# A gated recurrence and a sine MLP on one core: keys and queries transposed by DMA, weights cast by DMA on the Pool queue, decay factors kept in PSUM, gate phases in a new order on ACT

## The chip, the cores and the metric

The kernel runs on one core of one Trainium2 chip. The metric is the device time of one execution in microseconds (us). The core has five engines with instruction queues of their own: PE (matrix products), ACT (table functions), DVE and POOL (elementwise work) and SP (here only DMA issues). DMAs move data between HBM and SBUF, or within SBUF; matrix products land in PSUM.

## The reference

Four batches, eight heads, 768 steps and 48 dimensions per head. A recurrence per head keeps a 48x48 state that decays by a gate and takes in one outer product a step; its outputs, 3072 rows of 384, go through an MLP with a sine in the middle.

```python
f = 1.0 / (1.0 + np.exp(-f_logit))
for t in range(S):
    state = f[:, :, t, :, None] * state + np.einsum('bhd,bhe->bhde', k[:, :, t], v[:, :, t])
    y[:, :, t] = np.einsum('bhd,bhde->bhe', q[:, :, t], state)
...
h = x @ w_in                                 # 384 -> 2048
s = np.sin(alpha * h)
g = h + s * s / (alpha + 1e-09)
return (g @ w_out).astype(np.float32)        # 2048 -> 384
```

## The kernel before, in words

**Chunks and pairs.** The 768 steps are cut into 6 chunks of 128 (c = 0 to 5). A chunk of two batches, 16 heads, is a *pair* u = 2c or 2c + 1; there are 12. A pair's f, k, q and v come by one DMA each (`load`, 384 KB in pieces of 192 bytes), all on SP's queue in the order of the program, into rings of 3 buffers each. At most eight DMAs of a queue are under way, since the ninth waits for the first one's semaphore.

**The gate phase of a pair** (`pre`). ACT takes exp and ln of f (tiles `f`, `lf`, lines 317 and 320); PE forms running sums with a triangular mask (`cs`, line 342) and column sums (line 345); ACT takes exp of both signs, `Gi` (line 355) and `G` (line 351); then kh = k * Gi and qh = q * G (line 358, `mul`) are formed on POOL or DVE. exp and ln sit in another table of ACT than the sine, so each stretch of gate phases among the sines costs two table loads (line 602).

**Attention of a chunk and batch** (`attend`). PE transposes kh and qh, eight blocks of 128x128 (`tp`, line 398), DVE or ACT copies them to SBUF (`tr`, line 402), PE forms scores (`aps`, line 409), DVE masks them (`at`, line 413), PE adds the state's part (line 419) and the chunk's own (line 427) into `y`, and DVE or ACT casts that into `xT` (line 433), the MLP's input, transposed. `kv` and `st` (lines 439 to 447) carry the state to the next chunk; the decay for that is the last four columns of `G`. Heads are padded from 48 to 64 rows: xT has four blocks of 128 rows, and `spread` (line 474, six small DMAs on SP) moves the rows of block 1 into the gaps of the other three, so that the first layer needs three products. Chunk 0 isn't spread; it uses a fourth product with a weight tile `w_one_bf` of its own (line 495).

**The MLP** (`first`, `second`). Per 128 hidden features: `h` on PE (line 492), the sine on ACT (`s`, line 499), the square on POOL, DVE or ACT (`s2`, line 507), `g` on DVE (line 512). Chunk 0 goes in two halves of 256 columns, the others in 512. The second layer (`o`, line 528) sums 16 products per batch, then a copy (`osb`, line 536) and a store (line 539).

**The weights.** w_in comes in ten DMAs on the queues of SP and ACT as f32 into staging tiles `wi`, the rows of the heads in block 1 twice (for `w_one_bf`), 3.93 MB in all; w_out (3.15 MB) in four on SP. ACT and DVE cast them to bf16 (lines 273 and 289).

**What sets the order.** Every piece of work is an `Op` with a rank, a duration for each engine that may do it, the ops it depends on and the ring buffers it takes. `in_order` places them one by one: of all that could start, the one with the earliest start (plus `BIAS`), then the lowest rank. It writes the program of each engine; at run time each engine works its list off in that order and waits by semaphores. Two lists are fixed ahead: the loads, and `act_order`, the order of gate phases and sines on ACT. `MID` and `PRE34` say after which sine of chunks 0 and 1 a pair's gate phase comes; from chunk 1 on two pairs come after the eighth sine. `LAG` is the delay of the second layer's rank.

Of the kernel before, what the change touches and what calls it, by code (L numbers as in the profile page):

```python
# [16 lines left out]
N_H, N_A, NQ, NV, NG, LAG = 3, 3, 6, 4, 22, 10  # L17
SPX = "SP"
MID = {(0, 15): ([2], [-30]), (1, 7): ([3], [-20])}
PRE34 = ([4], [-10])  # L20
TR_ACT, Y_ACT = True, True
MULS = {"POOL": 1000, "DVE": 560}
BIAS = {"ACT": 600, "DVE": 200, "POOL": -300}
# [22 lines left out]
TABLE_LOAD, DMA_LATENCY, DMA_AHEAD = 1280, 1900, 4000  # L46


def in_order(ops, lines):
# [4 lines left out]
    dma_free, table = 0, None  # L54
# [23 lines left out]
    while left:  # L78
        best = None
        for o in pending:  # L80
# [5 lines left out]
            for e, dur in o.engs.items():  # L86
                s = max(t, free[e])
                if o.dma:
                    s = max(s, dma_free - DMA_AHEAD)
# [4 lines left out]
        if best is None:  # L94
            raise RuntimeError("no operation can start: " + "; ".join(
                f"{o.rank} {o.engs} {o.line and turn[o]} {nth} {[(n, len(b.ring.taken)) for b in o.takes for n in [b.ring.n]]}"
                for o in pending if SPX not in o.engs))
# [3 lines left out]
        if o.dma:  # L101
            dma_free = max(s + 600, dma_free) + o.dma
            o.end = dma_free + DMA_LATENCY
# [18 lines left out]
def kernel(  # L122
# [18 lines left out]

    nc = tc.nc
# [10 lines left out]
    BLK = (0, 2, 3)  # L153
# [12 lines left out]
    wst = pool("wst", 4)  # L166
# [14 lines left out]
    act_order, load_order = [], []  # L181

    def op(rank, engs, emit, deps=(), takes=(), holds=(), table=None, dma=None):
        o = Op(rank, engs, emit, [d for d in deps if d is not None], list(takes), table, dma)
        for b in list(takes) + list(holds):
# [5 lines left out]
        f=3, k=3, q=3, v=3, lf=2, qh=NQ, kh=NQ, vb=NV, G=6, Gi=4, a=N_A, tr=3, at0=3, at1=3, xT=2,  # L191
        h=N_H, s=3, s2=3, g=NG, o=2, osb=3, w=4).items()}
# [5 lines left out]
    qh_b = [consts.tile([C, HP, 2, E], BF16, name=f"qh{i}") for i in range(NQ)]  # L198
    kh_b = [consts.tile([C, HP, 2, E], BF16, name=f"kh{i}") for i in range(NQ)]
# [13 lines left out]
                            pattern=[[-1, FB]], channel_multiplier=1)  # L213
    ones_c = consts.tile([C, 1], BF16)
    nc.gpsimd.memset(ones_c, 1.0)
    for i in range(max(NQ, NV)):
        for ts in (lf_b, qh_b, kh_b, v_b):
            if i >= len(ts):
                continue
            if ts is v_b:  # L220
                nc.vector.memset(ts[i][:, :, :, 0:2, D:], 0.0)
                nc.vector.memset(ts[i][:, :, :, 2:4, 0:16], 0.0)
            else:
                t = ts[i] if ts is not lf_b else ts[i].rearrange("c p b r e -> c (p b) r e")
                nc.vector.memset(t.rearrange("c a r e -> c (a r) e")[:, :, D:], 0.0)
# [408 lines left out]
```

## Time and profile before

| | |
|---|---|
| median of 3 runs | 273.51 us (272.41 to 274.02) |
| the profiled execution | 272.08 us |
| its span, first to last instruction | 270.4 us |
| mean granted PE clock | 0.941 of full speed |
| busy: PE, DVE, ACT, POOL | 217.1, 171.0, 153.3, 139.7 us |
| DMA | 31.48 MB, of it 25.96 MB read from HBM |

A row of the profile is a group or a stretch. In a timeline the columns are start, time, engine, line, operation, result<-operands, count, and in brackets the idle time ahead of it with what ended it. In the chain of waits they are start, time, engine and line. In a group by shape the last column but one is busy time in all and mean ns of one instruction; PE's single durations overlap, so that runs of several in the chain (x8) tell more of their pace. Engine names with a q (SPq) are queues that issue DMAs; such a row lasts as long as the queue took for it, and grows when the rings are full. In the busy table by stretches the last three columns are the granted PE clock, the mean share of the 16 DMA engines in use, and GB/s.

### The profile page before, as it was taken

The numbers are of one execution on the slowest core, as the hardware profiler recorded it, in microseconds if no ns is written. First come the engines' busy times: TensorE is split into PE (matmuls) and PEld (weight loads), VectorE is DVE, ScalarE is ACT, GpSimd is POOL, SyncE is SP. The second block draws the span as 40 slices with busy tenths as digits, with TensorE's granted clock in tenths as the row PEclk, the third lists the DMA queues.
The fourth block names the chain that finished last, engine by engine and source line by source line (L and its number), as shares of the span: only waits on it lengthen the run. The fifth ranks groups of instructions, "written<-read, shape, count | busy, mean of one in ns | idle before, by whom it ended". The sixth has DMA issues, their size and how long they took to land.

```text
span 270.4 us, 4819 instructions
## 1 busy us (share of the span) xinstructions
PE 217.1 (80%) x1785; PEld 124.7 (46%) x1785; DVE 171.0 (63%) x296; ACT 153.3 (57%) x236; POOL 139.7 (52%) x154
## 2 busy tenths in 40 slices
PE   0650358896987879568999969999889999989994
PEld 0430235664564545244555545555555555435542
DVE  2661227768749777658766496856697667765641
ACT  4211475668276685594554975457956577555610
POOL 6400062656135456367428493547685656578830
PEclk9999999997599999975999986999979999999999
DMA  9999999999999669049920399710000001010111
GB/s 144 206 245 182 159 212 370 192 176 196 188 185 219 91 154 141 0 87 198 178 81 0 91 156 187 109 61 31 31 2 15 30 32 58 13 60 3 58 61 58
DMA packets 106295, 31.48 MB, mean 116 GB/s; under 512 B 100176, under 2 KB 105792, under 8 KB 105792
## 3 DMA queue, kind: packets, MB, share of 16 engines
q1 hardware_dynamic: 105920, 29.20, 59.5%
q10 hardware_dynamic: 320, 1.97, 3.5%
q8 instruction: 14, 0.23, 0.4%
q14 instruction: 9, 0.07, 0.1%
q0 software_dynamic: 32, 0.01, 0.0%
HBM read 25.96 MB, written 4.72 MB: 113 GB/s over the span
## 4 chain that ended last, share of the span: by engine, by line
PE 32%; DVE 15%; POOL 12%; ACT 11%; DMA 11%; issue 11%; SPq 5%; POOLq 1%; ACTq 0%; DVEq 0%
PE h L492 12%; POOL s L507 12%; PE o L528 9%; DVE qh L358 6%; DMA wi<-in_moe_w_in_dram 6%; SPq L237 4%; PE y L427 4%; DMA q<-in_q_dram 3%; DVE tr L402 3%; DMA v<-in_v_dram 3%; ACT lf L320 3%; ACT f L317 2%; ACT L602 2%; DVE at L413 2%; ACT s L499 2%
## 5 line engine op out<-in xcount | busy, mean ns | idle before, releaser
L507 POOL TENSOR_TENSOR s<-s 128x512 f32<-128x512 f32 (+1 forms) x112 | 102.3, 928 | 66.4 <-ACT s L499 63.6
L499 ACT ACTIVATE s<-h,al_p 128x512 f32<-128x512 f32 (+1 forms) x112 | 67.8, 626 | 50.7 <-PE h L492 37.5
L492 PE MATMUL h<-xT,w_in_bf 128*128 128x512 bf16 (+1 forms) x336 | 84.3, 365 | 15.2 <-ACT w_in_bf L273 8.9
L512 DVE SCALAR_TENSOR_TENSOR g<-s,al_r,h 128x512 bf16<-128x512 f32 (+1 forms) x112 | 73.4, 667 | 34.7 <-POOL s L507 33.7
L528 PE MATMUL o<-w_out_bf,g 128*128 128x384 bf16 x384 | 81.0, 327 | 1.5 <-DVE g L512 0.6
L358 POOL TENSOR_TENSOR kh<-k,Gi 128x384 bf16<-128x384 f32 x24 | 27.7, 1180 | 52.5 <-ACT Gi L355 52.5
L492 PEld LDWEIGHTS <-w_in_bf 128*128 128x128 bf16 x336 | 32.0, 101 | 42.4 <-ACT w_in_bf L273 10.7
L528 PEld LDWEIGHTS <-g 128*128 128x128 bf16 x384 | 36.1, 98 | 30.5 <-DVE g L512 2.5
L358 DVE TENSOR_TENSOR qh<-q,G 128x384 bf16<-128x384 f32 x19 | 21.8, 1189 | 21.1 <-ACT G L351 15.2
L413 DVE TENSOR_TENSOR at<-aps,mask 128x512 bf16<-128x512 f32 x48 | 30.8, 681 | 4.2 <-PE aps L409 4.0
L427 PE MATMUL y<-at,vb 128*64 128x128 bf16 x192 | 21.0, 261 | 2.2 <-DVE at L413 2.1
L602 ACT ACT_TABLE_LOAD x15 | 19.2, 1283 | 0.3
L433 ACT CAST xT<-y 128x512 bf16<-128x512 f32 x15 | 8.8, 585 | 18.5 <-PE y L427 18.1
L409 PE MATMUL aps<-tr 64*128 64x128 bf16 x192 | 13.4, 253 | 6.8 <-DVE tr L402 5.6
L427 PEld LDWEIGHTS <-vb 128*64 128x64 bf16 x192 | 13.7, 129 | 10.6 <-issue 9.2
L398 PE MATMUL tp<-ident,kh 128*128 128x128 bf16 x96 | 11.0, 248 | 7.8 <-POOL kh L358 6.2
L536 DVE COPY osb<-o 128x384 f32<-128x384 f32 x17 | 9.2, 553 | 9.4 <-PE o L528 9.3
L355 ACT ACTIVATE Gi<-cs 128x384 f32<-128x384 f32 x24 | 12.0, 499 | 4.4 <-PE cs L345 4.4
L409 PEld LDWEIGHTS <-tr 64*128 64x128 bf16 x192 | 7.2, 106 | 13.1 <-DVE tr L402 7.4
L495 PE MATMUL h<-xT,w_one_bf 128*128 128x256 bf16 x32 | 9.7, 304 | 3.4 <-DVE w_one_bf L273 3.4
L351 ACT ACTIVATE G<-cs 128x388 f32<-128x388 f32 x24 | 12.2, 510 | 0.0
L317 ACT ACTIVATE f<-f 128x768 f32<-128x768 f32 x12 | 10.1, 838 | 3.5 <-DMA f<-in_f_logit_dram 3.4
(53 smaller groups left out, 172.6 us busy)
## 6 DMA issues: line engine op xcount, KB each, us to landing
f<-in_f_logit_dram SPq DMA_DIRECT2D x12, 384.0 KB, 6.7
k<-in_k_dram SPq DMA_DIRECT2D x12, 384.0 KB, 6.7
q<-in_q_dram SPq DMA_DIRECT2D x12, 384.0 KB, 6.2
v<-in_v_dram SPq DMA_DIRECT2D x12, 384.0 KB, 6.7
out_dram<-osb SPq DMA_DIRECT2D x24, 192.0 KB, 1.9
wo<-in_moe_w_out_dram SPq DMA_DIRECT2D x4, 768.0 KB, 7.8
wi<-in_moe_w_in_dram SPq DMA_DIRECT2D x2, 512.0 KB, 9.3
wi<-in_moe_w_in_dram ACTq DMA_DIRECT2D x2, 512.0 KB, 9.9
```

Source lines behind the costliest of these rows:

```text
L317: nc.scalar.activation(out=tl["f", u], in_=tl["f", u], func=Act.Exp, scale=-1.0)
L351: nc.scalar.activation(out=tl["G", m], in_=tl["cs", m][:, :H * D + HP], func=Act.Exp, scale=-1.0)
L358: engine[e].tensor_mul(dst[bufs["qh" if dst is qh_b else "kh", m].place % NQ][:, :, :, :D], tl[n, u][:, i * H:(i + 1) * H, :].rearrange("c ...
L409: nc.tensor.matmul(aps[r][:, p, :], t[halves[r], p, :], t[halves[r], HP + p, :], start=True, stop=True)
L413: nc.vector.tensor_mul(a, tl[x, "a"][r], mask4)
L427: nc.tensor.matmul(tl[x, "y"][halves[r], p, :], v_b[bufs["vb", u].place % NV][:, i, r, p, :], tl[x, "at", r][:, p, :], start=(first and p ...
L492: nc.tensor.matmul(h[:, :n], w_in_bf[:, kb, fs], xT[:, BLK[kb], ts], start=(kb == 0), stop=(kb == KB - 1 and whole))
L499: nc.scalar.activation(out=s[:, :n], in_=tl[x, "h"][:, :n], func=Act.Sin, scale=al_p[:, fb:fb + 1])
L507: engine[e].tensor_mul(s2[:, :n], s[:, :n], s[:, :n])
L512: nc.vector.scalar_tensor_tensor(tl["g", c, fb][:, ts], tl[x, "s2"][:, :n], al_r[:, fb:fb + 1], tl[x, "h"][:, :n], Alu.mult, Alu.add)
L528: nc.tensor.matmul(tl["o", c, t], tl["g", c, fb][:, t * P:(t + 1) * P], w_out_bf[:, fb, :], start=(fb == 0), stop=(fb == FB - 1))
L602: nc.scalar.preload_act_table_set(now)
```

## The change

- **Transposes.** For chunks 1 to 5, `tp` on PE and the copy `tr` are replaced by one DMA on SP per chunk and batch (`dma_start_transpose`, 256 KB in bf16, from SBUF to SBUF), 20 in all. kh and qh now share one tile `qk`. Chunk 0 keeps PE.
- **Weights.** 20 DMAs on POOL's queue write bf16 straight into `w_in_bf` (16, by halves of the columns) and `w_out_bf` (4); staging tiles and casts go.
- **Chunk 0's fourth product.** Block 1's rows are placed by PE: shifted copies of the values (`v1_b`, formed by DVE) give three products per batch and half head in place of one (line 422 of the new kernel), so that xT of chunk 0 has three blocks and `w_one_bf` goes.
- **Decay factors.** `G` is written over `cs` in PSUM; the query product reads it there, now on DVE alone; a small copy `gl` keeps the four columns for the state. The last chunk forms no column sums.
- **Order.** `PHASES` lists how many sines stand between the gate phases of which pairs, `RANK` gives each pair's rank, attention has its own delay `ATT`, `LAG` grows from 10 to 50, the first-layer products are kept in order (`h_order`), and durations and biases are new.

The core of the diff:

```diff
-N_H, N_A, NQ, NV, NG, LAG = 3, 3, 6, 4, 22, 10
-MID = {(0, 15): ([2], [-30]), (1, 7): ([3], [-20])}
-PRE34 = ([4], [-10])
-MULS = {"POOL": 1000, "DVE": 560}
-BIAS = {"ACT": 600, "DVE": 200, "POOL": -300}
+N_H, N_A, NQ, NV, NG = 3, 3, 6, 4, 22
+LAG = 50
+ATT = 12
+PHASES = [("pre", [0]), ("sin", 1), ("pre", [1, 2]), ("sin", 21), ("pre", [3]), ("sin", 4), ("pre", [4]),
+          ("sin", 6), ("pre", [5, 6]), ("sin", 15), ("pre", [7]), ("sin", 15), ("pre", [8, 9]), ("sin",
+          6), ("pre", [10, 11]), ("sin", 44)]
+RANK = [-100, 26, -206, 68, -82, 12, -28, -12, 36, 24, 32, 16]
+MULS = {"POOL": 1180, "DVE": 1000}
+BIAS = {"ACT": 300, "DVE": 100, "POOL": -800}
...
-    dma_free, table = 0, None
+    dma_free, table = dict.fromkeys(("SP", "POOL"), 0), None
...
-        o = bufs[n, u].ready = op(rank, {SP: 500}, emit, takes=[bufs[n, u]], dma=2100)
+        o = bufs[n, u].ready = op(rank, {SP: 500}, emit, takes=[bufs[n, u]], dma=2500 if u < 2 else 2200)
...
+    def w_in_load(hf, rank):
+        for j, p0, r0, n in ((0, 0, 0, E), (1, 0, 80, E), (2, 16, 3 * D, D), (2, 0, D + 16, 16)):
+            for r in range(2):
+                def emit(e, j=j, p0=p0, r0=r0, n=n, r=r):
+                    nc.gpsimd.dma_start(out=w_in_bf[r * E + p0:r * E + p0 + n, j, HF[hf]],
+                                        in_=moe_w_in[4 * D * r + r0:4 * D * r + r0 + n, HF[hf]])
+                w_in_dma[hf].append(op(rank, {POOL: 1000}, emit, dma=1300 if n == E else 1000 if n == D else 500))
+
+    def w_out_load(rank):
...
+            def emit(e, gs=slice(4 * g4, 4 * g4 + 4)):
+                nc.gpsimd.dma_start(out=w_out_bf[:, gs, :], in_=src[:, gs, :])
...
             def G_(e, m=m):
-                tl["G", m] = at_pool.tile([P, H * D + HP], F32, tag="G", bufs=6, name=f"G_{m}")
-                nc.scalar.activation(out=tl["G", m], in_=tl["cs", m][:, :H * D + HP], func=Act.Exp, scale=-1.0)
+                g = tl["cs", m][:, :n_G]
+                nc.scalar.activation(out=g, in_=g, func=Act.Exp, scale=-1.0)
...
         def tr_(e):
-            t = tl[x, "tr"] = at_pool.tile([P, 2 * HP, C], BF16, tag="tr", name=f"tr_{c}_{b}")
+            t = tl[x, "tr"] = at_pool.tile([P, 2 * HP, C], BF16, tag="tr", bufs=4, name=f"tr_{c}_{b}")
+            if e == SP:
+                nc.sync.dma_start_transpose(t, qk_b[qkb.place % NQ].rearrange("c x p r e -> c (x p r e)"))
+                return
...
+                if first and p == 1:
+                    v1 = v1_b[u][:, i, r, :]
+                    vs = ((0, v1[:, 0:E]), (2, v1[:, E:2 * E]), (1, v1[:, 2 * E:]))
...
+            tr = op(rank, {SP: 1300}, tr_, deps=[made["kh", m], made["qh", m]], takes=[trb], holds=[qkb], dma=1000)
...
-            if not whole:
-                nc.tensor.matmul(h[:, :n], w_one_bf[:, fs], xT[:, 1, ts], start=False, stop=True)
...
-        a = op(rank, {PE: 430 if half else 645}, mm, deps=needs, takes=[hb], holds=[bufs["xT", c]])
+        a = op(rank, {PE: 330 if half else 645}, mm, deps=needs, takes=[hb], holds=[bufs["xT", c]])
+        a.line = "h"
+        h_order.append(a)
```

The programs that come out of it, at three places. In a tile's name the first number is the pair for f, k, q, v (tr_1_3, xT_1 and osb_0_1 name the chunk, then the batch), the last a running number. SP's queue ahead of chunk 1's spread, before:

```order
L237 DMA v_5_941<-in_v_dram 128x16x48
L237 DMA f_6_961<-in_f_logit_dram 128x16x48
L539 DMA out_0_dram<-osb_0_0_696 128x384
L539 DMA out_0_dram<-osb_0_1_698 128x384
L237 DMA k_6_1005<-in_k_dram 128x16x48
L237 DMA q_6_1040<-in_q_dram 128x16x48
L237 DMA v_6_1083<-in_v_dram 128x16x48
L474 DMA xT_1_832<-xT_1_832 16x512 x6
L237 DMA f_7_1204<-in_f_logit_dram 128x16x48
```

and the same place now:

```order
L240 DMA v_6_966<-in_v_dram 128x16x48
L389 DMA_TRANSPOSE tr_1_3_1004<-qk1_88 128x8x128
L240 DMA f_7_1014<-in_f_logit_dram 128x16x48
L538 DMA out_0_dram<-osb_0_1_758 128x384
L389 DMA_TRANSPOSE tr_2_0_1061<-qk2_89 128x8x128
L240 DMA k_7_1080<-in_k_dram 128x16x48
L240 DMA q_7_1114<-in_q_dram 128x16x48
L240 DMA v_7_1143<-in_v_dram 128x16x48
L389 DMA_TRANSPOSE tr_2_1_1188<-qk3_90 128x8x128
L473 DMA xT_1_945<-xT_1_945 16x512 x6
L240 DMA f_8_1254<-in_f_logit_dram 128x16x48
```

Pair 7's four loads, chunk 1's four transposes and the first two of chunk 2 have moved ahead of the spread: 28 loads stood there, now 32 with six transposes. The first transposes of chunk 1, tr_1_0 and tr_1_1, stand right behind v_5, the 24th load:

```order
L240 DMA f_5_693<-in_f_logit_dram 128x16x48
L240 DMA k_5_721<-in_k_dram 128x16x48
L240 DMA q_5_756<-in_q_dram 128x16x48
L240 DMA v_5_787<-in_v_dram 128x16x48
L389 DMA_TRANSPOSE tr_1_0_811<-qk4_91 128x8x128
L389 DMA_TRANSPOSE tr_1_1_820<-qk5_92 128x8x128
L240 DMA f_6_834<-in_f_logit_dram 128x16x48
```

Before, PE made them itself and needed nothing of SP there. ACT at chunk 1's first sine, before (the gate phase ahead of it is that of pair 4, whose tiles are 8 and 9):

```order
L602 ACT_TABLE_LOAD
L317 ACTIVATE f_4_693<-f_4_693 128x768
L320 ACTIVATE lf0_88<-f_4_693 128x4x4x48
L355 ACTIVATE Gi_8_1222<-cs_8_1208 128x384
L351 ACTIVATE G_8_1229<-cs_8_1208 128x388
L355 ACTIVATE Gi_9_1231<-cs_9_1215 128x384
L351 ACTIVATE G_9_1235<-cs_9_1215 128x388
L602 ACT_TABLE_LOAD
L499 ACTIVATE s_1_0_0_1243<-h_1_0_0_1194,al_p_151 128x512
```

and now (the end of a gate phase of pairs 5 and 6, tiles 10 to 13):

```order
L293 ACTIVATE f_6_834<-f_6_834 128x768
L296 ACTIVATE lf0_85<-f_6_834 128x4x4x48
L336 ACTIVATE Gi_10_1244<-cs_10_1221 128x384
L332 ACTIVATE cs_10_1221<-cs_10_1221 128x388
L336 ACTIVATE Gi_11_1256<-cs_11_1233 128x384
L332 ACTIVATE cs_11_1233<-cs_11_1233 128x388
L336 ACTIVATE Gi_12_1267<-cs_12_1248 128x384
L332 ACTIVATE cs_12_1248<-cs_12_1248 128x388
L336 ACTIVATE Gi_13_1285<-cs_13_1269 128x384
L332 ACTIVATE cs_13_1269<-cs_13_1269 128x388
L591 ACT_TABLE_LOAD
L496 ACTIVATE s_1_0_0_1300<-h_1_0_0_1281,al_p_136 128x512
```

Two more pairs' gate phases stand ahead of chunk 1's first sine. POOL's start, before:

```order
L215 MEMSET ones_c_119 128x1
L253 DMA al16_150<-in_moe_alpha_dram 16x128
L254 MEMSET wi3_149 128x2048
L358 TENSOR_TENSOR kh0_96<-k_0_157,Gi_0_184 128x8x48
L358 TENSOR_TENSOR kh1_97<-k_0_157,Gi_1_190 128x8x48
L358 TENSOR_TENSOR qh1_91<-q_0_159,G_1_193 128x8x48
```

and now:

```order
L258 DMA w_in_bf_134<-in_moe_w_in_dram 64x1024 x4
L258 DMA w_in_bf_134<-in_moe_w_in_dram 48x1024 x2
L343 TENSOR_TENSOR qk0_87<-k_0_140,Gi_0_173 128x8x48
L343 TENSOR_TENSOR qk1_88<-k_0_140,Gi_1_177 128x8x48
L258 DMA w_in_bf_134<-in_moe_w_in_dram 16x1024 x2
L258 DMA w_in_bf_134<-in_moe_w_in_dram 64x1024 x4
L258 DMA w_in_bf_134<-in_moe_w_in_dram 48x1024 x2
L258 DMA w_in_bf_134<-in_moe_w_in_dram 16x1024 x2
L504 TENSOR_TENSOR s2_0_0_0_325<-s_0_0_0_318 128x256
L266 DMA w_out_bf_135<-in_moe_w_out_dram 128x4x384 x3
L343 TENSOR_TENSOR qk2_89<-k_1_191,Gi_2_365 128x8x48
```

The weights' DMAs stand among POOL's products, six ahead of pair 0's keys and 13 more ahead of pair 1's.

More of the change, by code (lines that the diff above doesn't have):

```diff
@@ L94, in in_order @@
         if best is None:
[L95 to L97 removed]
+            raise RuntimeError("no operation can start")
         _, o, e, s, d = best
@@ L594 @@
+    assert n_sin == len(sins)
+    for c in range(NCH):
         for t in range(B):
```

228 lines of the change are left out of this document (100 added, 128 removed).

## The prediction

> **What bounds the kernel now.** I read the busy summary first, then the busy table by stretches of 10 us, then the chain of waits, and last the SP queue's own rows. In the summary one engine stands out:
>
> ```profile
> span 270.4 us, 4819 instructions
> PE 217.1 (80%) x1785; PEld 124.7 (46%) x1785; DVE 171.0 (63%) x296; ACT 153.3 (57%) x236; POOL 139.7 (52%) x154
> ```
>
> An 80% mean hides two regimes. The table by stretches has, in each row, the stretch, its length, the busy time of PE, PEld, DVE, ACT and POOL, then the granted PE clock, the mean share of the DMA engines and GB/s:
>
> ```profile
> 20.00:30.00 10.00, 0.79 (x2) 0.20 (x2) 1.39 (x2) 2.09 (x2) 0.00 (x0) 1.00 1.06 172
> ...
> 60.00:70.00 10.00, 6.84 (x73) 4.49 (x72) 8.09 (x14) 7.04 (x12) 4.13 (x5) 0.71 1.30 189
> ...
> 80.00:90.00 10.00, 7.70 (x107) 5.24 (x106) 8.77 (x16) 6.08 (x12) 4.63 (x6) 1.00 1.25 208
> ...
> 140.00:150.00 10.00, 10.00 (x55) 5.19 (x54) 5.53 (x9) 5.89 (x9) 7.50 (x8) 1.00 0.06 22
> 150.00:160.00 10.00, 7.82 (x79) 4.81 (x77) 6.80 (x9) 9.90 (x17) 6.05 (x6) 0.99 0.56 124
> ```
>
> To about 90 us the DMA engines are full (shares of 1.06 to 1.30) and PE has gaps; after that the DMA is nearly idle (0.06) and PE is full (10.00 of 10), but for a dip of 2.2 us where ACT does a gate block (150 to 160). So I price the first part in DMA time and the second in PE time. The border is the start of chunk 1's first layer, which the chain shows; its end is there too:
>
> ```profile
> 94.35 1.41 PE h L492 x6
> ...
> 261.35 5.37 PE o L528 x32
> ```
>
> It starts at 94.35, and 270.4 - 94.35 = 176.05 us follow, all of chunks 1 to 5.
>
> **First part: the DMA queue ahead of chunk 1.** Chunk 1's first layer needs the spread DMAs of xT_1, and these stand on SP's queue behind 28 loads before, and behind 32 loads, two stores and six transposes now (the rows of SP in the section on the change). A load's price is the distance of rows on SP's queue (start, time, instruction); from the first row to the end of the second there are 12 loads, and the others are the first load and the spread:
>
> ```profile
> 0.80 0.45 SPq L237 DMA_DIRECT2D f<-in_f_logit_dram  x1
> ...
> 52.52 2.05 SPq L237 DMA_DIRECT2D f<-in_f_logit_dram  x1
> ...
> 76.20 1.98 SPq L237 DMA_DIRECT2D v<-in_v_dram  x1
> ...
> 89.26 3.96 SPq L474 DMA_DIRECT2D xT<-xT  x6
> ```
>
> That is (76.20 + 1.98 - 52.52) / 12 = 2.14 us for 384 KB. The prices of the weights come from the casts that waited for w_in's second block (1 MB, two DMAs) and from the stretch with w_out's load in it:
>
> ```profile
> 16.86 1.04 ACT L273 CAST w_in_bf<-wi 128x1024 bf16<-128x1024 f32 x1 [6.96 <-DMA wi<-in_moe_w_in_dram]
> ...
> 21.45 1.04 ACT L273 CAST w_in_bf<-wi 128x1024 bf16<-128x1024 f32 x1 [3.54 <-DMA wi<-in_moe_w_in_dram]
> ```
>
> ```profile
> 42.00:44.00 2.00, 1.49 (x21) 1.07 (x19) 1.51 (x5) 1.97 (x3) 0.00 (x0) 1.00 1.07 387
> ```
>
> 1 MB in 21.45 - 16.86 = 4.59 us is 228 GB/s for w_in; w_out moved at up to 387. As a check on the kernel before: 0.8 + 28 x 2.14 + 3.93 MB of w_in at 228 (17.2) + 3.15 MB of w_out at 387 (8.1) + two stores of 192 KB at 189 GB/s (2.0) = 88.0, against the spread's 89.26. The queue's sum holds.
>
> The change, term by term. Loads: 32 x 2.14 = 68.5. w_in: 3.15 MB (block 1's rows are no longer read twice); no row shows a DMA that casts, so I bound it by the rate of w_in's own load (13.8 us) and by that of the 192-byte pieces of the loads, 189 GB/s (16.6); a gain is excluded, since the same bytes are read. I take 13.8, as it is the same read. w_out likewise lies between 8.1 and 16.6; I take 10, nearer to its own load. Transposes: no row has one. 256 KB take 0.7 us at 387 GB/s and 1.4 at 189; the far end is cutting into small pieces: a load's 2048 pieces in 2.14 us are 1.04 ns each, so 64-byte pieces (4096) would take 4.3. I take 1.4, since a 128x128 block's row (256 bytes) is nearest to a load's piece: 6 x 1.4 = 8.4. Stores 2.0. The spread itself about 2, between these rows' 1.8 and 3.96 above:
>
> ```profile
> xT<-xT SPq DMA_DIRECT2D x30, 16.0 KB, 1.8
> ```
>
> Sum: 0.8 + 68.5 + 13.8 + 10 + 8.4 + 2 + 2 = 105.5. Chunk 1's first layer starts 11 us later than before.
>
> The Trainium skill ("Advanced Engine Details and Errata", section X-Bar Transpose) says that on this chip such DMAs "are as fast as regular DMAs", 350 to 400 GB/s; an estimate from that is 0.7 us each, and by it the border would be 101.3. No run here shows it yet.
>
> Does the gate chain end even later? A gate block from table load to the next sine, and the pace of chunk 0's sines:
>
> ```profile
> 45.21 0.47 ACT L499 ACTIVATE s<-h,al_p 128x256 f32<-128x256 f32 x1 [1.24 <-PE h L495]
> ...
> 57.99 0.47 ACT L499 ACTIVATE s<-h,al_p 128x256 f32<-128x256 f32 x1 [0.74 <-POOL s L507]
> 58.48 1.28 ACT L602 ACT_TABLE_LOAD   x1
> ...
> 64.94 1.20 ACT L499 ACTIVATE s<-h,al_p 128x256 f32<-128x256 f32 x3
> ...
> 112.23 1.28 ACT L602 ACT_TABLE_LOAD   x1
> ...
> 121.23 1.84 ACT L499 ACTIVATE s<-h,al_p 128x512 f32<-128x512 f32 x3
> ```
>
> A block of one pair costs 6.5 us, of two 9.0, a half sine about 1.0 (13 from 45.21 to 57.99). On PE chunk 1's scores wait for the first transpose, which lands after 24 loads: 0.8 + 51.4 + 13.8 + 10 + 1.4 = 77.4; all that stands behind them on PE, the half layers from the tenth of the second half on, waits too. Then 3 us of scores and outputs, the block of pair 4 (6.5), six sines (6) and the block of pairs 5 and 6 (9.0): 102. So the DMA ends last, by 3.5 us, and ACT has done two pairs more than before.
>
> What else changes ahead of the border costs nothing there, the DMA being the cover: the casts of the weights leave ACT and DVE; POOL now issues 20 DMAs, and its one DMA of before took 0.7 us (20 of them between 20 x 0.7 = 14 us and, at the 2.14 of a full queue, 43 us; POOL's next products wait anyway for f_2, the ninth load, at 0.8 + 9 x 2.14 + 13.8 = 33.9); the fourth product per first-layer block goes (9.7 us on PE), against 16 more output products. If the DMA were no cover, these would be worth about 6 us of PE.
>
> ```profile
> L495 PE MATMUL h<-xT,w_one_bf 128*128 128x256 bf16 x32 | 9.7, 304 | 3.4 <-DVE w_one_bf L273 3.4
> ...
> L253 POOL DMA_DIRECT2D al<-in_moe_alpha_dram x1 | 0.7, 667 | 0.0
> ```
>
> **Second part: PE from the border on.** It was 176.05 us. The prices, from the chain's packed runs and the groups by shape:
>
> ```profile
> 128.92 0.68 PE tp L398 x8
> ...
> 160.15 0.64 PE y L419 x8
> 160.78 0.56 PE y L427 x4
> 161.34 0.58 PE aps L409 x8
> ```
>
> ```profile
> L442 PE MATMUL kv<-vb,kh 128*64 128x64 bf16 x160 | 8.0, 222 | 0.0
> L342 PE MATMUL cs<-lf,mask 128*128 128x384 bf16 x24 | 7.9, 351 | 3.0 <-ACT lf L320 2.6 <-ACT G L351 0.4
> ...
> L345 PE MATMUL cs<-ones_c,lf 128*128 128x1 bf16 x96 | 6.0, 166 | 0.0
> ...
> L439 PE MATMUL kv<-st,ident 128*128 128x256 bf16 x16 | 4.9, 309 | 0.0
> ```
>
> Sixteen sets of transposes (chunks 2 to 5) leave PE: 16 x 0.68 = 10.9. The last chunk's column sums go: 16 x 6.0 / 96 = 1.0. Work that now lies ahead of the border: six running sums (7.9 / 24 + 6.0 / 24 = 0.58 each) 3.5, two state products (8 x 8.0 / 160 + 4.9 / 16 = 0.71) 1.4, and one batch's scores and outputs (0.58 + 0.64 + 2 x 0.56) 2.3: 7.2 in all. Of gate blocks three are left behind the border where there were five; each left PE idle for up to 2.2 us (150 to 160), of 4.4 I take half. In all 10.9 + 1.0 + 7.2 + 2.2 = 21.3, which leaves 154.8. The copies of transposes that leave DVE and ACT, and the query products that go to DVE alone and read PSUM, lie beside PE (DVE 5.53 of 10 in 140 to 150) and count nothing. The later transposes count nothing either: SP's queue is nearly empty there (0.06), but without that cover each would delay scores by its landing.
>
> Span 105.5 + 154.8 = 260.3. The profiled execution took 272.08 us with its span of 270.4, so 1.7 lie around it: 262.0. The median of the three runs, 273.51, is 0.5% over that execution, so I forecast **263 us**, 3.8% less.
>
> **The rivals.** (a) *Transposes are dear, slower.* If a transpose holds the rings for 4.3 us, the six ahead of the spread add 6 x 2.9 = 17.4: 281 us. It decides from 3.1 us each on, where the 10 us of gain are gone. Against it: the pieces are as large as a load's; for it: no row shows the operation.
>
> (b) *Casting DMAs run at the rate of the small pieces, no change.* w_in and w_out at 16.6 each add 2.8 + 6.6 = 9.4: 272.5. For it: in 20 to 30 us, with two rings at work, only 172 GB/s moved; against it: w_out's 387.
>
> (c) *The rings add up, faster.* If POOL's transfers ran beside SP's, the border would be set by the gate chain and could stay at 94.35: 252. Against it: the same 172 GB/s, less than one ring's 228. The Trainium skill ("DMA: Bandwidth & Descriptors", section Issuing engines are not separate DMA queues) says that DMAs of all engines run on the same 16 DMA engines and interleave, so that a second issuer saves only issue time; by that rule (c) can't happen and the border stays at 105.5, and the 172 agrees.
>
> **How the numbers follow.** The forecast gets 0.52, with a range of its own of 254 to 271: down by faster transposes and the rest of the blocks' idle time, up by one or two stretches at a lower clock like 60 to 70 (0.71, 2.9 us each) after PE's waits. (a) gets 0.21, (b) 0.12, (c) 0.15. A measurement here can tell about 0.5% from no change. Faster by more: 0.50 of the forecast, 0.15 of (c), 0.04 of (b), 0.69. Within: 0.02, 0.06 of (b) and 0.01 of (a), 0.09. Slower: 0.02 of (b) and 0.20 of (a), 0.22. The range runs from (c) to (a), 252 to 281.
>
> **What would show it.** Right: DMA shares near 1 up to about 100 us, the spread of xT_1 issued near 102, chunk 1's first layer near 105 after a wait on DMA, PE busy total down by about 15 us, and some 155 us from there to the end. Wrong: a first layer of chunk 1 before 97 (the sum of the rings fails), a landing of transposes in a quiet stretch over 4 us, the weights' DMAs landing later than 55 us, or a PE that waits on transposes after 110 us.

## The result and the profile after

The changed kernel took 253.01 us (median of 4 runs, 252.5 to 256.46) against 272.96 (4 runs) for the kernel before in the same measurement: a ratio of 0.926, with a 95% interval of 0.921 to 0.931. One of the four runs, the one of 256.46, had a lower granted clock (0.930 against 0.946 to 0.952), and the ratio leaves it out. The forecast was 263, so the time fell by nearly twice as much as forecast (20.0 us instead of 10.5); it lies 1 us below the 254 to 271 given for the forecast itself and inside the whole range of 252 to 281. In what follows TensorE, ScalarE, VectorE, GpSimd and SyncE are other names for PE, ACT, DVE, POOL and SP.

The top of the page, the share of the DMA engines in 40 slices of 6.3 us, and the two DMA queues that matter:

```profile
span 250.8 us, 4495 instructions
PE 198.4 (79%) x1577; PEld 109.8 (44%) x1593; DVE 155.3 (62%) x306; ACT 140.3 (56%) x219; POOL 139.6 (56%) x168
...
DMA  8999999999999996999659802897640001100021
...
q1 hardware_dynamic: 124608, 29.34, 69.3%
q0 software_dynamic: 3168, 3.16, 8.0%
```

Of the two regimes the first stands as forecast: the DMA engines are full to 94 us (15 slices). Behind that they aren't nearly idle, but busy, with gaps, to about 185. PE is busy 18.7 us less than before (217.1). The border (the start of chunk 1's first layer), on PE's timeline, and the spread that it waited for, on SP's queue:

```profile
98.06 0.61 PE L491 MATMUL h<-xT,w_in_bf 128*128 128x512 bf16 x1 [2.01 <-DMA xT<-xT]
```

```profile
94.26 3.76 SPq L473 DMA_DIRECT2D xT<-xT  x6
```

Chunk 1's first layer starts at 98.06 instead of the forecast's 105.5, 7.4 us early; 250.8 - 98.06 = 152.7 us follow it, against 154.8, 2.1 early. The border before was 94.35, so the whole gain lies behind it: 176.05 - 152.7 = 23.3 us, less 3.7 for the later border. ScalarE's gate block (a gate phase with the table loads around it) of pairs 5 and 6, its first and last rows, and the first sine of chunk 1:

```profile
89.40 1.28 ACT L591 ACT_TABLE_LOAD   x1
...
97.66 1.28 ACT L591 ACT_TABLE_LOAD   x1
100.46 0.69 ACT L496 ACTIVATE s<-h,al_p 128x512 f32<-128x512 f32 x1 [1.52 <-PE h L491]
```

The block ends at 97.66 + 1.28 = 98.9, and the sine waits 1.5 us more for the first layer. So the DMA ends last, and ScalarE's block ends 1.5 us before the sine can start. From the spread's issue to the end, before and after (the columns are those of the table by stretches: PE, PEld, DVE, ACT, POOL, granted clock, DMA share, GB/s):

```profile
89.26:270.40 181.14, 161.78 (x1290) 88.35 (x1287) 120.98 (x186) 108.79 (x166) 106.17 (x103) 0.94 0.38 73
```

```profile
94.26:250.80 156.54, 140.82 (x1043) 73.09 (x1056) 105.79 (x177) 90.58 (x139) 96.51 (x94) 0.96 0.51 98
```

PE's busy time fell by 21.0 us and its idle time from 19.4 to 15.7. I use this row, from the spread's issue on, for every run below: it splits each time into a part ahead of the spread and a part behind it.

### The profile page after: what moved, and what is told of

It reads as the page before. It is cut to its first block, busy times and chain, and to the rows that moved or that the text cites. A ratio compares the mean times of both kernels' runs of the same rounds, so it can differ in the third digit from the quotient of the medians.

```text
span 250.8 us, 4495 instructions
## 1 busy us (share of the span) xinstructions
PE 198.4 (79%) x1577; PEld 109.8 (44%) x1593; DVE 155.3 (62%) x306; ACT 140.3 (56%) x219; POOL 139.6 (56%) x168
## 3 DMA queue, kind: packets, MB, share of 16 engines
q0 software_dynamic: 3168, 3.16, 8.0%
## 4 chain that ended last, share of the span: by engine, by line
PE 35%; POOL 18%; issue 15%; SPq 10%; DMA 9%; DVE 7%; ACT 4%; POOLq 0%; ACTq 0%; DVEq 0%
POOL s L504 16%; PE o L527 16%; PE h L491 14%; SPq L240 9%; DMA f<-in_f_logit_dram 5%; DMA v<-in_v_dram 3%; DVE g L509 2%; PE y L422 2%; POOL qk L343 2%; DVE at L402 2%; PE aps L398 1%; ACT Gi L336 1%; SPq L473 1%; ACT L591 1%; DVE osb L535 1%
## 5 line engine op out<-in xcount | busy, mean ns | idle before, releaser
L527 PE MATMUL o<-w_out_bf,g 128*128 128x384 bf16 x384 | 82.2, 334 | 0.1
L491 PEld LDWEIGHTS <-w_in_bf 128*128 128x128 bf16 x336 | 33.1, 103 | 37.9 <-issue 12.7
L343 POOL TENSOR_TENSOR qk<-k,Gi 128x384 bf16<-128x384 f32 x24 | 23.5, 1005 | 39.4 <-ACT Gi L336 39.3
L323 PE MATMUL cs<-lf,mask 128*128 128x384 bf16 x24 | 8.4, 366 | 14.9 <-ACT lf L296 12.9
L422 PE MATMUL y<-at,vb 128*64 128x128 bf16 x184 | 18.9, 239 | 1.1 <-DVE at L402 0.7
L429 ACT CAST xT<-y 128x512 bf16<-128x512 f32 (+1 forms) x13 | 7.4, 567 | 17.3 <-PE y L422 17.3
L422 PEld LDWEIGHTS <-vb 128*64 128x64 bf16 x184 | 12.3, 119 | 10.3 <-issue 9.3
L340 DVE COPY gl<-cs 128x4 f32<-128x4 f32 x20 | 3.2, 159 | 21.3 <-ACT cs L332 21.3
L535 DVE COPY osb<-o 128x384 f32<-128x384 f32 x19 | 10.5, 556 | 9.0 <-PE o L527 8.7
L343 DVE TENSOR_TENSOR qk<-q,cs 128x384 bf16<-128x384 f32 x24 | 12.9, 546 | 2.9 <-DMA q<-in_q_dram 2.9
L326 PEld LDWEIGHTS <-lf 128*128 128x128 bf16 x80 | 5.0, 102 | 16.3 <-issue 15.1
## 6 DMA issues: line engine op xcount, KB each, us to landing
w_in_bf<-in_moe_w_in_dram POOLq DMA_DIRECT2D x8, 128.0 KB, 5.8
```

The costliest lines, as they stand in the source:

```text
L343: engine[e].tensor_mul(qk_b[bufs["qk", m].place % NQ][:, "kq".index(n), :, :, :D], tl[n, u][:, i * H:(i + 1) * H, :].rearrange("c (r p) d ...
L422: nc.tensor.matmul(tl[x, "y"][halves[r], blk, :], v_, tl[x, "at", r][:, p, :], start=(first and p == 0), stop=True, skip_group_check=True)
L491: nc.tensor.matmul(h[:, :n], w_in_bf[:, kb, fs], xT[:, kb, ts], start=(kb == 0), stop=(kb == KB - 1))
L527: nc.tensor.matmul(tl["o", c, t], tl["g", c, fb][:, t * P:(t + 1) * P], w_out_bf[:, fb, :], start=(fb == 0), stop=(fb == FB - 1))
```

## The experiments

Theory: the border is the sum of all DMA time ahead of chunk 1's spread, on whichever queue it is issued, with ScalarE's gate block close behind; after it PE's work counts. Rivals: the border is a chain of gate phases that begins when f of pair 2 lands; the gain is the new order's alone; it is the weights' or the transposes' alone. All diffs are against the changed kernel and are shown in short: lines are left out, and `...` stands for arguments left out.

**Which work sets the border.** Half of w_in left out:

```
-                    nc.gpsimd.dma_start(out=w_in_bf[...], in_=moe_w_in[...])
+                    if hf: return
+                    nc.gpsimd.dma_start(out=w_in_bf[...], in_=moe_w_in[...])
-        fs = slice(fb * P, (fb + 1) * P)
+        fs = slice(fb % 8 * P, (fb % 8 + 1) * P)
```

> The DMAs of the second half of w_in are left out (eight of sixteen); the second half of the hidden features takes the first half's columns, so TensorE, ScalarE and VectorE do as much as ever. My theory, that the sum of the DMA time of both rings ahead of the spread of chunk 1 sets the border: w_in costs about 9 us of DMA time in all (not the 13.8 of the forecast), half of it 4.5 us, and the first layer of chunk 1 starts at 93.5 to 95 instead of 98.1; time 248 to 250 us. If the price were the forecast's, 6.9 us: 246 us. Rival, that ScalarE's order (the gate block of pairs 5 and 6, which ends at 98.9) sets the border whatever the DMA does: within 1 us of 253.

With this edit the output isn't the reference's. Measured: 248.97 us, spread at

```profile
89.28 3.75 SPq L475 DMA_DIRECT2D xT<-xT  x6
```

4.98 us earlier, and 4.0 us reached the end. If the other half costs as much, w_in costs 10.0 us in all. The gate block moved with it here (it ended at 94.2 instead of 98.9). The last quarter of w_out left out, which leaves everything up to the first gate blocks as it is:

```
-                nc.gpsimd.dma_start(out=w_out_bf[:, gs, :], in_=src[:, gs, :])
+                if gs.start < 12:
+                    nc.gpsimd.dma_start(out=w_out_bf[:, gs, :], in_=src[:, gs, :])
-                nc.tensor.matmul(..., w_out_bf[:, fb, :], ...)
+                nc.tensor.matmul(..., w_out_bf[:, fb % 12, :], ...)
```

> The last quarter of w_out isn't loaded (one DMA on the Pool queue, issued at 44.8 us); the second layer takes the third quarter again in its place, so every engine does as much as before, but the output isn't the reference's. It takes DMA time away only behind 35.9 us, where the gate block of pairs 1 and 2 starts. My theory, that the border is the sum of all DMA time ahead of it: a quarter of w_out costs 2.5 us, the spread of chunk 1 goes out at 91.8 instead of 94.3, 250.5 us. Rival, that the border is a chain of gate phases, sines and attention that starts when the f of pair 2 lands (the half of w_in left out made that landing earlier too): spread at 94.3, 253 us.

The spread and the end of ScalarE's block:

```profile
91.63 3.76 SPq L474 DMA_DIRECT2D xT<-xT  x6
```

```profile
96.36 1.28 ACT L592 ACT_TABLE_LOAD   x1
97.66 0.69 ACT L497 ACTIVATE s<-h,al_p 128x512 f32<-128x512 f32 x1
```

The spread came 2.63 us earlier, as the sum says, and not at the rival's 94.3. The first sine came 2.8 us earlier (97.66 instead of 100.46); it now starts the moment the gate block ends, with no wait for PE. But the time is 252.08, only 0.9 less than 253.01. The lead is lost behind the border: the last table load of the last gate block stands at 176.32 instead of 176.75, 0.4 us earlier. What takes it there isn't shown. This run's row, and the changed kernel's:

```profile
176.32 1.28 ACT L592 ACT_TABLE_LOAD   x1
```

```profile
176.75 1.28 ACT L591 ACT_TABLE_LOAD   x1
```

The same bytes at another time:

```
+    seq = in_order(...)
+    for g4 in (2, 1):
+        move(w_out_dma[g4], made["kh", 5])
```

> The second and third quarter of w_out are issued on the Pool queue behind the key products of pair 2 instead of ahead of the key products of pair 1; nothing else moves on any engine. The f of pair 2 should land 4 to 5 us earlier than 35.9, with the same bytes moved ahead of the border. My theory (sum of DMA time): border unchanged, spread of chunk 1 within 1 us of 94.3, 252 to 254 us. Rival (chain that starts at that landing): spread near 89.5, 248 to 249 us.

252.96 us. The f of pair 2 was used at 31.73 instead of 35.88, and nothing came of it:

```profile
31.73 0.84 ACT L293 ACTIVATE f<-f 128x768 f32<-128x768 f32 x1 [5.56 <-DMA f<-in_f_logit_dram]
```

```profile
93.71 3.78 SPq L473 DMA_DIRECT2D xT<-xT  x6
```

The spread moved by 0.55 us only. The chain that starts at that landing is refuted; the sum of DMA time holds.

**What a transpose by DMA costs.** Each issued twice:

```
+                tj = at_pool.tile(..., tag="trj", bufs=4)
+                nc.sync.dma_start_transpose(tj, qk_b[...])
                 nc.sync.dma_start_transpose(t, qk_b[...])
```

> Each transpose by DMA is issued twice, the first time into a tile that nobody reads; all else as changed. Six of the twenty lie ahead of the border. My theory, at 1.5 us of DMA time each: 9 us more ahead of the border, first layer of chunk 1 at 106 to 108, and nothing after it: 260 to 263 us. If a transpose cost 4.3 us (the upper bound of the forecast), 26 us: near 279. If 0.7, 4 us: 257. Rival, that ScalarE's order sets the border and the DMA has slack: within 2 us of 253.

268.82 us, more than the 260 to 263 of the theory. The spread went out at 102.13, 7.87 us later for six transposes more: 1.31 us each, near the 1.4 of the sum. But I had expected nothing behind the border, and there it lost 9.0 us more (165.57 against 156.54 from the spread on). What PE waited for there (in a row of the waits: who waited for what, us in total, times, the longest):

```profile
PE h L493 <- DMA xT<-xT: 6.5, 3, 4.9
PE aps L400 <- DMA tr<-qk: 5.8, 3, 3.2
```

Of the first row the longest, 4.9 us, is the border's own wait (2.0 in the changed kernel); in the changed kernel the waits of the second row come to 0.9 us. So the DMA isn't empty behind the border. It wasn't before the change either: the DMA shares of the kernel before, in 40 slices of 6.8 us, and two of its stretches of 10 us show it full at 120 to 130 and at 160 to 170.

```profile
DMA  9999999999999669049920399710000001010111
...
120.00:130.00 10.00, 8.56 (x80) 5.25 (x80) 8.34 (x14) 5.28 (x8) 7.11 (x7) 0.54 1.12 169
...
160.00:170.00 10.00, 9.86 (x95) 5.38 (x95) 7.57 (x15) 4.51 (x7) 5.79 (x7) 0.67 1.44 187
```

Chunk 1 transposed on TensorE instead (the condition `first` of the two branches becomes `first or c == 1`):

> The changed kernel with the keys and queries of chunk 1 alone transposed on TensorE (4 of 20). My theory: 4 x 1.3 = 5.2 us of DMA time fewer ahead of the border, where TensorE has idle time for 4 x 0.68 us, so the spread goes out at 89 to 91 instead of 94.3; since the gate block of pairs 5 and 6 then sets the border (2.6 us less DMA gave 0.9 us), 250.5 to 253. Rival, that evictions on ScalarE and VectorE and TensorE's slower clock there eat it: 254 us or more.

251.21 us, ratio 0.918 (0.912 to 0.925): the best median of all, though its interval overlaps the changed kernel's. The spread went out 7.0 us earlier, at 87.24 and not at the expected 89 to 91: in the order that the planner makes of this edit, one transpose is left ahead of it instead of six (5 x 1.31 = 6.6 us). Only 1.8 us came of it, since here the gate block set the first sine, 2.1 us earlier than in the changed kernel (end of the block 97.09 + 1.28, first sine 98.39):

```profile
87.24 5.15 SPq L473 DMA_DIRECT2D xT<-xT  x6
```

```profile
97.09 1.28 ACT L591 ACT_TABLE_LOAD   x1
98.39 1.84 ACT L496 ACTIVATE s<-h,al_p 128x512 f32<-128x512 f32 x3
```

**Can the loads stand behind the spread instead?** Seven loads moved (`move` as above: k, q, v of pair 6 behind chunk 1's fourth transpose, the loads of pair 7 behind the spread, the cast of pair 6's values behind chunk 1's last outputs):

> On SyncE's queue the loads of k, q and v of pair 6 go out behind the fourth transpose of chunk 1 instead of ahead of it, and the four loads of pair 7 behind the spread of chunk 1; the cast of pair 6's values on VectorE stands behind the last evacuation of chunk 1's outputs; nothing else moves. That takes 7 x 2.08 = 14.6 us of DMA time from ahead of the border. My theory (sum of DMA time, with ScalarE's gate block of pairs 5 and 6 nearly as late): the spread goes out at 84 to 89 instead of 94.3, and the gate block, which waited for sines behind the attention, ends 2 to 4 us earlier than 98.9: 249 to 252 us. Rival, that the gate block alone sets the start of chunk 1's sines: 252.5 to 253.5. Rival, that the loads are then missed later: 255 us or more.

261.14 us, 8 more than without the move: the last rival. The spread went out at 91.11, not at 84 to 89. Only the four loads of pair 7 stand behind it now; those of pair 6 still go out ahead of it. The queue had issued everything else by 84.8, and then the spread waited for the last cast of chunk 1's attention outputs:

```profile
SPq L474 <- DVE xT L429: 6.2, 1, 6.2
```

So DMA time isn't the only limit of the spread. Chunk 1's attention is another, whose last cast in the changed kernel is done at 91.20 + 0.69 = 91.9, 2.4 us before the spread goes out:

```profile
91.20 0.69 DVE L429 CAST xT<-y 128x512 bf16<-128x512 f32 x1 [1.25 <-PE y L422]
```

The loss lies behind the border. In VectorE's list one cast stood ahead of the query products and waited:

```profile
105.46 0.36 DVE L302 CAST vb<-v 128x384 bf16<-128x384 f32 x1 [10.24 <-DMA v<-in_v_dram]
```

With that cast (the values of pair 7) behind chunk 1's seventh feature block too:

> As the run with seven loads behind (261.1 us), and the cast of pair 7's values on VectorE is moved behind the seventh feature block of chunk 1, so that VectorE no longer stands 10 us for a load at 95. Theory, that this one wait was the loss: 249 to 252 us. Rival, that the DMA engines stay full up to 120 us, so that loads put off there are missed by the next cast in VectorE's order (pair 8's values, due at 112): 254 to 260 us.

259.53 us: the rival held. The 10 us wait on VectorE was not all. A transpose of chunk 2 now stands in the queue behind the postponed loads, and PE waited 7.7 us for it:

```profile
PE aps L398 <- DMA tr<-qk: 8.7, 2, 7.7
```

A load put off is no load saved: here it delayed what came next on the queue.

**What the transposes were worth on PE.** Chunks 3 to 5 transposed on TensorE (`first or c >= 3`):

> Keys and queries of chunks 3, 4 and 5 transposed on TensorE again (12 of the 20 that the changed kernel does by DMA), all else as changed. My theory, that the stretch after the border is bound by TensorE's own work: each set costs the 0.68 us of eight transposes of the kernel before, 12 x 0.68 = 8.2 us, and the DMAs taken away there are worth nothing: 261 us (259.5 to 263), border unchanged near 98. Rival, that the gain comes from the new order and the transposes lay beside other work: 253 to 255 us. Rival, that a transpose on TensorE also costs the waits for its eviction and its PSUM buffer: over 264 us.

263.16 us, 10.2 more and just over the theory's range, with the border where it was (spread at 93.65). From there on:

```profile
93.65:260.70 167.05, 149.05 (x1140) 80.27 (x1150) 114.29 (x189) 92.02 (x139) 96.40 (x94) 0.94 0.37 73
```

PE is busy 8.23 us more, 0.69 for each of twelve sets, the forecast's price (a set is the eight transposes of a chunk and batch); 2.3 us more of idle time come on top. PE's waits put only 0.2 us of idle time down to an eviction, and most of the rest to VectorE's gate copies and products; which work of VectorE's was in the way isn't shown. A set is worth 0.88.

**The decay factors.** Back in SBUF, and the query products on either engine:

```
-                nc.scalar.activation(out=cs[:, :n_G], in_=cs[:, :n_G], func=Act.Exp, scale=-1.0)
+                nc.scalar.activation(out=G[:, :n_G], in_=cs[:, :n_G], func=Act.Exp, scale=-1.0)
-            made["qh", m] = op(rank + i, {DVE: 600}, qm, ..., holds=[qb_, cb])
+            made["qh", m] = op(rank + i, MULS, qm, ..., holds=[qb_, glb])
```

> The decay factors of the queries go to SBUF again, and the products of the queries to VectorE or GpSimd; transposes, weights and order as changed. My theory: these products (0.55 us on VectorE from PSUM, 1.0 to 1.2 from SBUF) lie beside DMA and TensorE work, so only the last products ahead of the border count, 0 to 1.5 us: 253 to 254.5 us. Rival, that this part carries several us of the gain because 24 products shorter by 0.6 us (15 us of VectorE and GpSimd) free the engines on which masks and second layers wait: 257 us or more.

257.37 us, 4.4 more: the rival held. The same product before and after this edit, first from SBUF on either engine, then from PSUM (mean ns in the last but one place):

```profile
L339 POOL TENSOR_TENSOR qk<-q,G 128x384 bf16<-128x384 f32 x17 | 19.2, 1138 | 3.5 <-DMA q<-in_q_dram 3.5
...
L339 DVE TENSOR_TENSOR qk<-q,G 128x384 bf16<-128x384 f32 x7 | 9.2, 1319 | 8.1 <-DMA q<-in_q_dram 5.5 <-ACT G L332 2.6
```

```profile
L343 DVE TENSOR_TENSOR qk<-q,cs 128x384 bf16<-128x384 f32 x24 | 12.9, 546 | 2.9 <-DMA q<-in_q_dram 2.9
```

The products no longer share GpSimd with the squares of the sines and take 546 ns instead of 1138 to 1319; whether PSUM or GpSimd's work beside them makes the difference wasn't separated. The loss lies behind the border (162.43 from the spread on, against 156.54; the planner also placed other work anew there, so the 4.4 is of products and placing together).

**The weights.** Float loads, staging tiles and casts on ScalarE and VectorE, as before:

```
-                    nc.gpsimd.dma_start(out=w_in_bf[...], in_=moe_w_in[...])
+                engine[e].dma_start(out=wi[j][...], in_=moe_w_in[...])
+                (nc.scalar.copy or nc.vector.tensor_copy)(w_in_bf[:, j, HF[hf]], wi[j][:, HF[hf]])
```

> The weights go to float staging tiles by the queues of SyncE and ScalarE again and are cast to bf16 on ScalarE and VectorE (six casts of w_in, four of w_out), the four staging tiles being shared by w_in and w_out as before; transposes, decay and order as changed. My theory: the same bytes are read, so the border moves only by what the loads wait for staging tiles, and 10 us of casts lie beside DMA work: 252 to 257 us. Rival, that the casting DMA carries several us because the casts and the staging tiles held the order of the first part up: 260 us or more.

267.09 us, 14.1 more: the rival held. The spread went out at 103.63, 9.4 us later. On SP's queue, from w_in's first DMA to the first of w_out, with the four loads of pair 1 between:

```profile
6.64 3.77 SPq L261 DMA_DIRECT2D wi<-in_moe_w_in_dram  x4
11.48 0.38 SPq L241 DMA_DIRECT2D f<-in_f_logit_dram  x1
...
31.54 5.53 SPq L281 DMA_DIRECT2D wo<-in_moe_w_out_dram  x4
```

31.54 - 6.64 - 4 x 2.08 = 16.6 us for w_in as float, with ScalarE's queue helping, against 10.0 with the cast in the DMA. That is 6.6 of the 9.4 us, and SP's queue waited for a landing of w_in for 5.4 us within it; the other 2.8 aren't assigned. The rest of the loss (4.9 us) lies behind the spread, 3.0 us of it at the border: the first sine of chunk 1 started at 112.80, straight behind a gate block, 12.3 us later than in the changed kernel.

```profile
111.50 1.28 ACT L613 ACT_TABLE_LOAD   x1
112.80 1.84 ACT L515 ACTIVATE s<-h,al_p 128x512 f32<-128x512 f32 x3
```

**The order.** Gate phases, ranks and distances of before, with the decay factors in SBUF (so it stands against 257.4 us):

```
-LAG = 50
-ATT = 12
-PHASES = [("pre", [0]), ("sin", 1), ("pre", [1, 2]), ("sin", 21), ...]
+LAG = 10
+ATT = 20
+PHASES = [("pre", [0]), ("pre", [1]), ("sin", 16), ("pre", [2]), ("sin", 8), ...]
```

> The order of before: its gate phases, ranks, and the second layers and attention placed by the old distances (10 and 20); transposes and weights by DMA as changed, and the decay factors of the queries in SBUF, as in the run that has only this undone (257.4 us), with which it is to be compared. My theory: the 7.2 us of work that the new order moved ahead of the border and the 2.2 us of two gate blocks come back, border within 3 us of the 93.5 at which the spread went out there: 264 to 268 us. Rival, that the new order gives nothing of itself and the transposes and weights carry the whole: 256 to 259 us. Rival, that the order carries more, since it also sets when VectorE and ScalarE let TensorE wait: 270 us or more.

298.85 us, 41 more than with the new order and 26 more than the kernel before. The spread went out at 94.82, so the border hardly moved. From there:

```profile
94.82:298.30 203.48, 156.73 (x1068) 76.36 (x1067) 108.51 (x165) 94.35 (x145) 99.77 (x94) 0.88 0.42 76
```

```profile
PE h L486 <- DMA xT<-xT: 13.4, 10, 4.7
PE aps L393 <- DMA tr<-qk: 7.0, 3, 3.3
PE h L486 <- DVE g L504: 6.9, 12, 3.0
```

PE was idle for 46.8 us there, 28 more than with the new order (18.4), and it was busy for 12.7 us more, in part with work that lies behind the border again, in part, it may be, because the mean clock was 0.88 instead of 0.93; the two weren't separated. The distance of the second layers alone back at 50 in the old order, and alone at 20 in the new one:

> As the run with the old order (298.9 us), but the second layers stand at the new distance of 50 behind the first layers instead of 10, so that they rank behind all other work and fill TensorE's gaps; gate phases, ranks and the place of attention stay old, decay factors in SBUF. Theory A, that the 41 us between the old and the new order come from that distance, since second layers ranked early make TensorE wait for features of VectorE while attention could run: 256 to 270 us. Theory B, that they come from the gate phases and from attention ranked where its transposes by DMA land too late (TensorE waited 7.0 us for them there, 8.1 us for spreads): above 285 us.

> The changed kernel with a distance of 20 instead of 50 between first and second layers; gate phases, ranks and attention's place as changed. Theory A (the distance is what the new order gains by): 262 us or more. Theory B (the gate phases and attention's place are): 252 to 257 us.

298.16 and 254.2 us: theory B both times. Does the old order lose by itself? With all transposes on TensorE again (`first` becomes `True`), so that of the change the weights alone remain:

> The run with the old order (298.9 us), but with all keys and queries transposed on TensorE as before: of the change, the weights cast by DMA remain (with the second blocks' rows laid out for it, and no column sums in the last chunk); decay factors in SBUF, old gate phases, ranks and distances. Theory, that transposes by DMA need the new order and lose in the old one: 260 to 268 us, that is the kernel before less the 9 us that casting DMAs take from the first part, and the transposes by DMA cost the old order some 35 us. Rival, that the old order itself loses under this planner (its times for DMA and products were changed too): 285 us or more.

272.1 us, ratio 0.998 (0.994 to 1.003). Both my numbers missed. The transposes by DMA cost the old order 26.8 us, so it loses only with them. And the spread did go out 5.0 us earlier than before, at 84.29, but nothing came of it: chunk 1's sines began at 96.75 instead of 99.07, held by the gate block of pair 4 (which ended at 96.74), and the stretch from the spread on was 4.6 us longer than before (185.71).

The parts together, in us. Every row but the first also has the change's products of chunk 0, its last chunk without column sums, and its planner's durations:

| order | transposes of chunks 1 to 5 | weights | decay | time |
|---|---|---|---|---|
| old | TensorE | cast on engines | SBUF | 273.0 (before) |
| old | TensorE | by DMA | SBUF | 272.1 |
| old | DMA | by DMA | SBUF | 298.9 |
| new | DMA | by DMA | SBUF | 257.4 |
| new | DMA | by DMA | PSUM | 253.0 (changed) |
| new | DMA | cast on engines | PSUM | 267.1 |
| new | DMA, 3 to 5 TensorE | by DMA | PSUM | 263.2 |
| new | DMA, 1 TensorE | by DMA | PSUM | 251.2 |

The new order with all transposes on TensorE was not run, so what the order is worth by itself stays open.

## Why the prediction was wrong

The direction and the first regime were right: a sum of DMA time ahead of the spread, on both queues, sets chunk 1's first layer. The size failed, 9.5 us in the span, and 7.4 of them are the first part's sum. The second part came out near its forecast by terms that cancel, which is luck.

- **The border, 105.5, was 98.1.** The term that failed is w_in's 13.8 us, taken from the read rate of a plain float load (228 GB/s): it measured 2 x 4.98 = 10.0, below its lower bound, for which I had said that a gain is excluded. A load measured 2.08 instead of 2.14 (32 x 0.06 = 1.9 us), a transpose 1.31 instead of 1.4 (0.5 us), and w_out 4 x 2.63 = 10.5 instead of 10. Together 5.7 us. The sum had the spread itself going out at 103.5, and it went out 9.2 us earlier, at 94.26, while the step from there to the first layer took 3.8 us instead of 2. So 3.5 us of the way to the spread aren't assigned. A part may be that the issue runs ahead of the rings: when the spread went out, the DMA still had about 2 us of work (share 1.31 from 94 to 96 us, 0.10 from 96 to 98). The load's price comes from four loads in a row with no weights left to move:

```profile
56.62 1.98 SPq L240 DMA_DIRECT2D f<-in_f_logit_dram  x1
...
64.93 4.37 SPq L389 DMA_TRANSPOSE tr<-qk  x2
```

  (64.93 - 56.62) / 4 = 2.08.
- **The check of the sum on the kernel before, 88.0 against 89.26, was in part luck.** There the last load had left the queue at 87.2, and the spread waited for ScalarE's cast of chunk 1's last attention output. Its first sine, at 99.07, came straight behind the gate block of pair 4 (97.78 + 1.28), so that before the change DMA was not the last limit.

```profile
SPq L474 <- ACT xT L433: 1.9, 1, 1.9
```

- **The gate chain, estimated at 102, ended at 98.9.** That DMA ends last and the chain is close to it was right, and it is why 7.0 us less ahead of the spread gave only 1.8 with chunk 1's transposes on TensorE. With a quarter of w_out left out the chain moved along, and the 2.6 us were lost elsewhere.
- **Behind the border, 154.8, was 152.7.** The total was nearly right, its terms were not. Sixteen sets of transposes were priced at 10.9 by PE's own time; the run with twelve of them back gives 0.88 each, 14.1 for sixteen as an estimate. The decay factors, "count nothing", were 4.4 with the placing that goes with them. The new order was priced by what it moves, 7.2 + 2.2. With transposes by DMA it was worth 41 us (298.9 against 257.4), and only with it did the transposes gain; whether it gains without them wasn't measured.
- **"The later transposes count nothing", since SP's queue is nearly empty there,** was read from one row of the trace before, 140 to 150 us. Its neighbours, shown above, had shares of 1.12 and 1.44, and from the spread on the mean share was 0.38 before and 0.51 after. Doubling the transposes cost 9.0 us behind the border.
- **Rival (c), 252 us, had the nearest time and the wrong mechanism.** The queues share one budget of DMA time, so POOL's transfers don't come free beside SP's: half of w_in and a quarter of w_out on the Pool queue moved the spread by 4.98 and 2.63 us, six transposes on SP's by 7.87. The Trainium skill ("DMA: Bandwidth & Descriptors", section Issuing engines are not separate DMA queues) says that DMAs run on the same 16 DMA engines whoever started them, and these runs agree. Rivals (a), 4.3 us for a transpose, and (b), casting at 189 GB/s, fall with 1.31 and 10.0.
- **What would show it.** DMA shares of 9 tenths to 94 us, 152.7 us after the border and PE's busy time down (18.7 against "about 15") came as listed; the spread (94.3, not 102) and the first layer (98, not 105) came too early, though not before 97. Of the signs listed against it, one came, and it was small: behind 110 us PE waited for a transpose once, for 0.95 us. The weights had landed by 50.4 us, and the last four transposes, behind 172 us, landed within 3.0 to 3.3 us.

## What to carry to other kernels

Price a new DMA by bounds that reach below the nearest row as well: a plain load was no lower bound for one that casts. When a change swaps a short wait for a long one (here TensorE's transposes for transposes by DMA that land 3 to 6 us after their issue), don't price its new order as work moved: the same swap cost 27 us in the old order and belongs to the gain only with the new one. Where several limits lie within about 2 us of each other, here the DMA sum, a gate block and chunk 1's attention, easing one of them gains about the distance to the next. And read how busy a queue is from all the stretches that the argument covers, not from one row.

## What the hardware showed unexpectedly

- A DMA that casts f32 to bf16 moved half of w_in (1.57 MB read) in 4.98 us of ring time, 316 GB/s; a quarter of w_out (0.79 MB read) took 2.63, 299 GB/s. The plain float load of w_in took 16.6 us of queue time for the whole 3.15 MB, 190 GB/s. For the Pool queue the page counts 3.16 MB, the size of both weights in bf16, half of what was read. Why the cast makes the same read cheaper isn't shown.
- A transpose of 256 KB by DMA took 1.31 us of ring time, 200 GB/s, about the rate of the loads in 192-byte pieces (384 KB in 2.08 us, 189 GB/s). Twenty more of them added 21120 packets and 5.24 MB to the queue, 1056 packets of 248 bytes each:

```profile
q1 hardware_dynamic: 145728, 34.58, 78.6%
```

  The Trainium skill ("Advanced Engine Details and Errata", section X-Bar Transpose) calls them as fast as regular DMAs, 350 to 400 GB/s, by which an estimate is 0.7 us. Beside this case's own loads (189 GB/s) the first half agrees with the 200 measured; the rate isn't reached in these runs, from SBUF to SBUF.
- PE's granted clock fell to a half in stretches that follow PE's pauses. In the changed kernel it was full to 70 us, then had means of 0.66 and 0.68:

```profile
60.00:70.00 10.00, 6.62 (x55) 3.94 (x52) 4.95 (x14) 7.89 (x14) 5.50 (x8) 1.00 1.36 190
70.00:80.00 10.00, 9.62 (x98) 6.25 (x100) 7.14 (x16) 6.14 (x10) 2.37 (x4) 0.66 1.29 172
80.00:90.00 10.00, 6.20 (x57) 3.60 (x55) 6.89 (x16) 6.08 (x12) 5.60 (x8) 0.68 1.29 188
```

  In stretches of 1 us of the same trace it is 0.50 for 6.8 us at a time, from 70.0, 83.6, 97.3 and 128.0 us on, each within 2 us of a stretch of 0.8 us or more in which PE did almost nothing (68 to 69, 83 to 84, 96 to 98, 127 to 128). Not every pause does this: from 30 to 40 us PE was busy for 1.79 us, and the clock stayed at 1.00. So idle time on PE can be paid twice. In the old order with transposes by DMA 28 us more of idle time came with 12.7 us more of busy time, over the 7.2 us of work that the forecast counted as moved; how much of that is the clock wasn't separated.
